# Linear attention and a one-expert MoE on one Trainium2 core: attention of each sequence placed about one MoE ahead of its own, w1 slot copy split over f, a weight load no longer ordered behind the last copies

## The chip, the cores and the metric

The kernel runs on one core of a Trainium2 chip. The metric is device time in microseconds of one execution. Engines are named as in the profile: PE does the matrix products (PEld its weight loads), DVE, ACT and POOL the elementwise work, SP issues transfers. A transfer issued from SP shows in the profile as queue q1, one from POOL as q0.

## What is computed

Eight sequences of 576 positions, eight heads of 64. The attention is linear (softmax over the features of q, softmax over the positions of k), and its result is the input of a mixture of experts in which one expert is chosen for each whole sequence:

```python
q_s = softmax(q, axis=-1)
k_s = softmax(k, axis=positions)
kv  = einsum('bhsd,bhse->bhde', k_s, v)
x   = einsum('bhsd,bhde->bhse', q_s, kv)          # -> (8, 576, 512)
logits = x.mean(axis=1) @ w_gate                  # 8 experts
e = argmax(logits); gate = softmax(logits)[e]     # one expert for each sequence
out = gate * (relu(x @ w1[e]) @ w2[e])            # w1 512x1024, w2 1024x512
```

For the inputs of these runs the experts of the eight sequences are 2, 3, 3, 1, 3, 3, 4, 6.

## The kernel before

**Halves and steps.** Attention is done in halves: half n belongs to sequence b = n // 2 and holds four heads, as two groups g of two heads each. For a half, ACT takes exp of q and k (`exp_q`, `exp_k`, L124, L136), POOL casts v to fp16 (`cast_v`, L132), DVE sums q over the features and takes the reciprocals (`scale_q`, L142, L144), and POOL multiplies them in (L145; DVE for the first halves). `kvt_step` then runs on PE the 18 small products of k and v (L160) and 18 transposes of q (L181). DVE takes both out of PSUM (`kv_out`, L168 and L170; `t_out`, L189). `x_step` multiplies them for one group (L219, L220), and one DVE instruction takes the result out and sums it for the gate (L230). There is one PSUM buffer for these products, which the gate's small products use too, so each x step waits until DVE has read the one before.

**Gate and weights.** `gate_step` (L261) multiplies the pooled x with w_gate (L265), and DVE finds the expert and whether one of the last sequences had it (L270 to L297). There are five slots for weights, and sequence b owns slot b % 5. POOL reads the expert's number and issues four transfers from the fp32 weights in DRAM to the fp16 slot: two for w1 (L315) and two for w2 (L327). Where the expert lies in a slot already, their condition is false and they move nothing. `gate_exp`, `gate_split` and `gate_spread` make the gate's weight and bring it to all partitions (L343, L348 to L351, L359 to L362). `fetch` (L365) copies, on DVE, the slot that holds the expert into the slot of the sequence, in two parts for w1 and two for w2 (L374); where the weights were just loaded it copies the slot onto itself. So for each sequence the MoE's weights pass through these four copies.

**The MoE.** `moe(b)` (L384) is a Python generator of 17 units. Units 0 to 7 make 128 rows of the hidden layer each (L393 for 512 positions, L398 for the other 64; ACT applies relu, L402). Units 8 to 15 are the four output tiles of 128 positions in two pieces each (L412), and ACT multiplies by the gate (L419). Unit 16 is the last 64 positions (L427).

**What sets the order.** Every engine runs its instructions in the order in which the program writes them (`manual_schedule`). A table of ticks sets it: sequence b's MoE takes ticks 17 b to 17 b + 17, one for each unit, and an entry `at(t, ...)` with t from 17 b + m up to 17 b + m + 1 is written right behind unit m of `moe(b)`. Attention of sequence 0, and of 1 but for two x steps, is written ahead of all MoEs. For b from 2 on, the table puts `kvt_step` of its two halves at two places, the x steps 2 and 4 ticks later, `exp_q` and `cast_v` 5.4 ticks ahead, `exp_k` and the input load of half n + 3 4.4 ahead, and `scale_q` 4.2 ahead. The gate follows the second half. The input tiles have three buffers, so the load of half n + 3 waits for the exps and the cast of half n. SP issues those loads and the stores of the output, in order.

Of the kernel before, what the change touches and what calls it, by code (L numbers as in the profile page):

```python
# [19 lines left out]
def kernel(  # L20
# [15 lines left out]
    nc = tc.nc  # L36
# [9 lines left out]
    NS = 5  # L46
# [61 lines left out]

    out_p = out.rearrange("b (p j) d -> b p j d", j=J)

    ins, halves, seqs, issued = {}, {}, {}, {}

    def load(n, names="qkv"):
        if n >= 2 * B:
# [19 lines left out]
    def exp_k(n):  # L134
        ek = e_pool.tile([128, J, 2, Dh], FP16, name="ek")
        nc.scalar.activation(out=ek.rearrange("p j n d -> p n j d"), in_=ins.pop((n, "k")), func=AF.Exp)  # L136
        halves[n]["ek"] = ek
# [123 lines left out]
    def gate_step(b):  # L261
# [103 lines left out]
    def fetch(b, w_all, part):  # L365

        if "src" not in seqs[b]:
            seqs[b]["src"] = nc.values_load(
                seqs[b]["sidx"][0:1, 0:1], engines=[ET.DVE], min_val=0, max_val=NS - 1,
                skip_runtime_bounds_check_because=IN_RANGE,  # L370
            )
        half = w_all.shape[2] // 2
        cs = slice(part * half, (part + 1) * half)
        copy = nc.vector.tensor_copy(  # L374
            out=w_all[:, b % NS, cs],
            in_=w_all[:, ds(seqs[b]["src"], 1), cs].rearrange("p o c f -> p (o c) f"),
        )
        for load_inst in issued.get(b + 1, ()):
            tc.declare_no_dep(
                copy.ins, load_inst.ins,  # L380
                reason="the slot that b + 1 loads into is taken out of the history before b looks for its source",
            )

    def moe(b):  # L384
        xt = seqs[b]["xt"]
# [72 lines left out]
    at_gate(2, 1)  # L458
    for b in range(2, B):
        u = 20 if b == 2 else 33 + 14 * (b - 3)  # L460
        for i in range(2):
            n, t = 2 * b + i, u + i * (8 if b == 2 else 5)
            at(t, kvt_step, n)
            for g in range(2):
                at(t + 2 + 2 * g, x_step, n, g)
            at(t - 5.4, exp_q, n)
            at(t - 5.4, cast_v, n)
            at(t - 4.4, exp_k, n)
            if n + 3 < 2 * B:
                at(t - 4.4, load, n + 3)  # L470
            at(t - 4.2, scale_q, n, nc.gpsimd)
# [23 lines left out]
    with tc.manual_schedule(engines={ET.PE, ET.DVE, ET.Activation, ET.Pool, ET.SP}):  # L495
# [75 lines left out]
```

## Time and profile before

| what | value |
|---|---|
| median of three runs | 228.77 us (226.83 to 229.58) |
| the profiled execution, its own time | 228.89 us |
| its span | 227.2 us |
| PE, DVE, ACT, POOL busy | 181.5, 118.0, 112.9, 60.6 us |
| PE idle before the hidden layer's products (L393), put down to DVE's copies (L374) | 18.4 us in 6 waits |
| weight transfers (q0), moved | 10.49 MB, five experts of 2.1 MB in fp16 |
| input loads and stores (q1), moved | 37.76 MB |

The span is what the profile shows between the first and the last instruction; the execution's own time is 1.7 us longer. Only sequences 0, 1, 3, 6 and 7 move weights. A row of the timeline gives the start in us, the time from its first to its last instruction, the engine and line, and in brackets how long the engine sat idle before it and what ended that.

### The profile page before, as it was taken

The page shows a single profiled execution, that of the slowest core. Times are in us where ns is not written, and L with a number is a line of the kernel's source. Part 1 is how long each engine was busy: PE and PEld are TensorE (multiplying, and loading weights), DVE is VectorE, ACT ScalarE, POOL GpSimd, SP SyncE. Part 2 cuts the span into 40 slices and gives each one's busy share as a digit, 9 for nine tenths or more (in the row PEclk, how much of TensorE's full clock was granted, in tenths as well). Part 3 has the DMA queues.
Part 4 walks back from the last instruction along what each step waited for, and adds up shares of the span by engine and source line. Part 5 has one row for each costly group of instructions (what it writes and reads, how often), then busy time and mean ns, then how long its engine had stood idle before and what let it go on. Part 6 is the DMA issues. An engine that isn't in the chain of part 4 may idle for free.

```text
span 227.2 us, 4594 instructions
## 1 busy us (share of the span) xinstructions
PE 181.5 (80%) x1703; PEld 96.1 (42%) x1703; DVE 118.0 (52%) x365; ACT 112.9 (50%) x177; POOL 60.6 (27%) x70
## 2 busy tenths in 40 slices
PE   6376599958999399965393996969898978999990
PEld 6353345423555145432151444544445533545440
DVE  0848824043548965673244876777699655220000
ACT  3785755462595134662035462845538432645541
POOL 1235403330254150267000334045137313000000
PEclk9755569996999769988599799999999996999999
DMA  6997999999999990399995569372425999965044
GB/s 201 379 390 283 145 251 297 183 235 351 398 400 401 373 316 4 100 300 201 289 285 142 198 182 282 109 264 52 106 54 75 194 250 183 208 122 131 0 107 102
DMA packets 28582, 48.55 MB, mean 214 GB/s; under 512 B 2960, under 2 KB 10128, under 8 KB 28560
## 3 DMA queue, kind: packets, MB, share of 16 engines
q1 hardware_dynamic: 19472, 37.76, 49.9%
q0 software_dynamic: 8544, 10.49, 28.5%
q8 instruction: 13, 0.21, 0.4%
q10 hardware_dynamic: 544, 0.02, 0.1%
q14 instruction: 9, 0.07, 0.1%
HBM read 61.88 MB, written 9.44 MB: 314 GB/s over the span
## 4 chain that ended last, share of the span: by engine, by line
PE 43%; DVE 22%; DMA 20%; ACT 5%; issue 5%; POOL 1%; DVEq 1%; POOLq 0%; ACTq 0%
DMA w_all<-in_moe_w_dram 16%; PE mm L393 16%; PE mm L412 15%; DVE qs L142 5%; DVE w_all L374 4%; PE kv L160 3%; DVE same L279 2%; PE x L219 2%; ACT eq L124 2%; PE ht L398 2%; DMA k_in<-in_k_dram 2%; DVE kv L170 2%; DMA q_in<-in_q_dram 2%; PE mm L427 2%; DVE xt L230 2%
## 5 line engine op out<-in xcount | busy, mean ns | idle before, releaser
L393 PE MATMUL mm<-xt,w_all 128*128 128x512 f16 x256 | 74.3, 421 | 18.9 <-DVE w_all L374 18.4
L402 ACT ACTIVATE hsb<-mm 128x512 f16<-128x512 f32 x64 | 37.6, 593 | 56.8 <-PE mm L393 56.7
L412 PE MATMUL mm<-w_all,hsb 128*128 128x512 f16 x256 | 60.9, 385 | 0.1
L145 POOL TENSOR_TENSOR eq<-eq,qsi 128x1152 f16<-128x1152 f16 x13 | 27.5, 2116 | 72.8 <-DVE zz L270 39.0
L393 PEld LDWEIGHTS <-w_all 128*128 128x128 f16 x256 | 21.7, 104 | 43.0 <-DVE w_all L374 23.5
L419 ACT ACTIVATE osb<-mm,gate 128x512 f32<-128x512 f32 x32 | 21.9, 684 | 29.3 <-PE mm L412 25.3
L412 PEld LDWEIGHTS <-hsb 128*128 128x128 f16 x256 | 23.5, 99 | 27.0 <-issue 1.7
L374 DVE COPY w_all<-w_all 128x2048 f16 x28 | 21.1, 754 | 22.4 <-DMA w_all<-in_moe_w_dram 21.3
L142 DVE TENSOR_REDUCE qs<-eq 128x18 f32<-128x1152 f16 x16 | 21.5, 1346 | 13.9 <-ACT eq L124 13.9
L230 DVE CUSTOM_DVE_ANT_0 xt<-x,ones_f 128x576 f16<-128x576 f32 x26 | 19.4, 746 | 18.0 <-PE x L220 18.0
L398 PEld LDWEIGHTS <-w_all 128*128 128x128 f16 x256 | 17.7, 104 | 18.2 <-issue 5.6
L132 POOL CAST va<-v_in 128x1152 f16<-128x1152 f32 x14 | 16.3, 1162 | 21.9 <-DMA v_in<-in_v_dram 21.7
L124 ACT ACTIVATE eq<-q_in 128x1152 f16<-128x1152 f32 x16 | 18.5, 1156 | 2.1 <-DMA q_in<-in_q_dram 2.0
L219 PE MATMUL x<-qt,kv 128*128 128x512 f16 x32 | 14.5, 452 | 6.2 <-DVE pooled L230 4.3
L398 PE MATMUL ht<-xt,w_all 128*128 128x64 f16 x256 | 19.2, 201 | 0.0
L136 ACT ACTIVATE ek<-k_in 128x1152 f16<-128x1152 f32 x16 | 18.5, 1158 | 0.8 <-DMA k_in<-in_k_dram 0.8
L315 POOL DMA_DIRECT2D w_all<-in_moe_w_dram x18 | 8.3, 463 | 31.0 <-DVE hl L350 24.1
L160 PEld LDWEIGHTS <-ek 64*128 64x128 f16 x288 | 10.4, 105 | 11.8 <-issue 8.0
L160 PE MATMUL kv<-va,ek 64*128 64x129 f16 x270 | 12.1, 236 | 2.7 <-ACT qt L187 2.3
L168 DVE RECIPROCAL icv<-kv 128x1 f32<-128x1 f32 x30 | 4.9, 162 | 13.1 <-PE kv L181 11.9
L170 DVE SCALAR_TENSOR_TENSOR kv<-kv,icv,blkmask 128x128 f16<-128x128 f32 x30 | 10.5, 351 | 1.1
L189 DVE COPY qt<-kv 128x576 f16<-128x576 f16 x24 | 10.7, 448 | 0.0
(80 smaller groups left out, 138.2 us busy)
## 6 DMA issues: line engine op xcount, KB each, us to landing
w_all<-in_moe_w_dram POOLq DMA_DIRECT2D x30, 512.0 KB
q_in<-in_q_dram SPq DMA_DIRECT2D x16, 576.0 KB, 7.0
k_in<-in_k_dram SPq DMA_DIRECT2D x16, 576.0 KB, 9.4
v_in<-in_v_dram SPq DMA_DIRECT2D x16, 576.0 KB, 9.1
out_dram<-osb SPq DMA_DIRECT2D x64, 128.0 KB, 5.1
w_all<-in_moe_w_dram POOLq DMA_DIRECT2D x4, 256.0 KB
out_dram<-osb_t SPq DMA_DIRECT2D x16, 64.0 KB, 3.3
wg_sb<-in_moe_w_gate_dram ACTq DMA_DIRECT2D x2, 8.0 KB, 5.1
```

The source lines that it names most:

```text
L124: nc.scalar.activation(out=eq.rearrange("p j n d -> p n j d"), in_=ins.pop((n, "q")), func=AF.Exp)
L142: nc.vector.tensor_reduce(out=qs, in_=eq, op=ALU.add, axis=AX.X)
L145: eng.tensor_tensor(out=eq, in0=eq, in1=qsi.unsqueeze(3).to_broadcast([128, J, 2, Dh]), op=ALU.mult,)
L160: nc.tensor.matmul(kps[g][:, 0:129], lhsT=ek[r, j], rhs=va[r, j], start=(j == 0), stop=(j == J - 1),)
L219: nc.tensor.matmul(px[:, 0:SM], lhsT=kvs[g], rhs=qts[g][:, 0:SM], start=True, stop=True)
L230: nc.vector.tensor_tensor_reduce(out=xt[:, c, :], in0=px[:, 0:S], in1=ones_f32.to_broadcast([128, S]), scale=1.0, scalar=0.0, op0=ALU.mult ...
L374: copy = nc.vector.tensor_copy(out=w_all[:, b % NS, cs], in_=w_all[:, ds(seqs[b]["src"], 1), cs].rearrange("p o c f -> p (o c) f"),)
L393: nc.tensor.matmul(phm, lhsT=w1_sb[:, c, fsl], rhs=xt[:, c, 0:SM], start=(c == 0), stop=(c == ND - 1),)
L398: nc.tensor.matmul(pht[:, fc * ST:(fc + 1) * ST], lhsT=w1_sb[:, c, fsl], rhs=xt[:, c, SM:S], start=(fc == 0 and c == 0), stop=(fc == NF - ...
L402: nc.scalar.activation(out=hsb[:, fc, 0:SM], in_=phm, func=AF.Relu)
L412: nc.tensor.matmul(po, lhsT=hsb[:, fc, st * 128:st * 128 + 128], rhs=w2_sb[:, fc, :], start=(fc == 0), stop=(fc == NF - 1),)
L419: nc.scalar.mul(osb, po, gate)
```

## The change

The table of ticks is written anew. The places of `kvt_step` for b = 2 to 7 go from (20, 28), (33, 38), (47, 52), (61, 66), (75, 80), (89, 94) to (15, 25), (30, 35), (41, 46), (58, 64), (74, 80), (91, 97). The MoEs of these sequences stay at ticks 34, 51, 68, 85, 102 and 119. The gate goes from 5 to 5.5 ticks behind the second half, and its three later steps from 1, 2 and 4 ticks behind it to 3, 4 and 6. The input loads of halves 5 and 6 go from tick 14 to 9.5. The copies of w2 go from 1 and 2 ticks behind the MoE's start to 4 and 5. In the copies of w1 the two parts are now the two halves of the hidden layer (f), where they were the two halves of the input features (c). The weight loads of sequence b are declared free of the copies of b - 1, where the program writes those copies first. Ahead of the MoEs, `exp_k(2)` goes ahead of an x step.

```diff
+        for load_inst in issued[b]:
+            for copy in copies.get(b - 1, ()):
+                apart(load_inst, copy)
+
+    def apart(first, second):
+        tc.declare_no_dep(
+            first.ins, second.ins,
+            reason="the slot that b + 1 loads into is taken out of the history before b looks for its source",
+        )
...
-        half = w_all.shape[2] // 2
-        cs = slice(part * half, (part + 1) * half)
+        if w_all is w1_all:
+            cs, fs = slice(0, ND), slice(part * (F // 2), (part + 1) * (F // 2))
+        else:
+            cs, fs = slice(part * (NF // 2), (part + 1) * (NF // 2)), slice(0, D)
         copy = nc.vector.tensor_copy(
-            out=w_all[:, b % NS, cs],
-            in_=w_all[:, ds(seqs[b]["src"], 1), cs].rearrange("p o c f -> p (o c) f"),
+            out=w_all[:, b % NS, cs, fs],
+            in_=w_all[:, ds(seqs[b]["src"], 1), cs, fs].rearrange("p o c f -> p (o c) f"),
         )
+        copies.setdefault(b, []).append(copy)
...
         at(t, gate_step, b)
-        at(t + 1, gate_exp, b)
-        at(t + 2, gate_split, b)
-        at(t + 4, gate_spread, b)
+        at(t + 3, gate_exp, b)
+        at(t + 4, gate_split, b)
+        at(t + 6, gate_spread, b)
...
+    at(9.5, load, 5)
+    at(9.6, load, 6)
+    places = [(15, 25), (30, 35), (41, 46), (58, 64), (74, 80), (91, 97)]
     for b in range(2, B):
-        u = 20 if b == 2 else 33 + 14 * (b - 3)
         for i in range(2):
-            n, t = 2 * b + i, u + i * (8 if b == 2 else 5)
+            n, t = 2 * b + i, places[b - 2][i]
...
-        at_gate(t + 5, b)
+        at_gate(places[b - 2][1] + 5.5, b)
     for b in range(1, B):
         for part in range(2):
-            at(NU * b - 0.8 + 0.2 * part, fetch, b, w1_all, part)
-            at(NU * b + 1 + part, fetch, b, w2_all, part)
-    at(14, load, 5)
-    at(14, load, 6)
+            at(NU * b - 1 + 0.5 * part, fetch, b, w1_all, part)
+            at(NU * b + 4 + part, fetch, b, w2_all, part)
...
         exp_q(2)
+        exp_k(2)
         x_step(1, 0)
-        exp_k(2)
         x_step(1, 1)
```

**On DVE, ahead of the copies of w1 for sequence 2.** Before, DVE ends that sequence's gate (nmx is its last instruction) and takes half 6 out of PSUM (icv, kv and qt for two groups) before it reads the slot's number (sidx) and copies:

```order
L297 TENSOR_SCALAR nmx_1148<-mx8_1132 1x1
L168 RECIPROCAL icv_1198<-kv_1160 128x1
L170 SCALAR_TENSOR_TENSOR kv_1200<-kv_1160,icv_1198,blkmask_93 128x128
L189 COPY qt_1202<-kv_1160 128x576
L168 RECIPROCAL icv_1204<-kv_1161 128x1
L170 SCALAR_TENSOR_TENSOR kv_1206<-kv_1161,icv_1204,blkmask_93 128x128
L189 COPY qt_1208<-kv_1161 128x576
L368 TENSOR_LOAD sidx_1144
L374 ISA
L374 COPY w1_all_119<-w1_all_119 128x2048
```

Now half 6 stands ahead of the gate, and between the gate and the copies stand the sums and reciprocals of half 7 (qs, qsi), whose product POOL then makes, and one x step of half 6 (xt):

```order
L297 TENSOR_SCALAR nmx_1164<-mx8_1148 1x1
L142 TENSOR_REDUCE qs_1184<-eq_1080 128x18
L144 RECIPROCAL qsi_1186<-qs_1184 128x18
L230 ISA xt_1202,pooled_1203<-x_1204,ones_f32_97 128x576
L230 ISA pooled_1203 128x1
L377 TENSOR_LOAD sidx_1160
L385 ISA
L385 COPY w1_all_119<-w1_all_119 128x4x512
```

What moved: kv and qt went ahead of the gate, and a sum with its product and an x step came in behind it, directly ahead of the copies.

**On SP, from the output of the first MoE on.** Before, the stores of three tiles (osb) go first, and then the inputs of halves 5 and 6:

```order
L421 DMA out_0_dram<-osb_717 64x512 x2
L421 DMA out_0_dram<-osb_730 64x512 x2
L421 DMA out_0_dram<-osb_743 64x512 x2
L119 DMA q_in_752<-in_q_dram 128x2x576
L119 DMA k_in_754<-in_k_dram 128x2x576
L119 DMA v_in_756<-in_v_dram 128x2x576
L119 DMA q_in_758<-in_q_dram 128x2x576
```

Now the inputs of halves 5, 6 and 7 follow the first tile, ahead of the other stores:

```order
L430 DMA out_0_dram<-osb_717 64x512 x2
L119 DMA q_in_721<-in_q_dram 128x2x576
L119 DMA k_in_723<-in_k_dram 128x2x576
L119 DMA v_in_725<-in_v_dram 128x2x576
L119 DMA q_in_727<-in_q_dram 128x2x576
L119 DMA k_in_729<-in_k_dram 128x2x576
L119 DMA v_in_731<-in_v_dram 128x2x576
L119 DMA q_in_743<-in_q_dram 128x2x576
L119 DMA k_in_745<-in_k_dram 128x2x576
L119 DMA v_in_747<-in_v_dram 128x2x576
L430 DMA out_0_dram<-osb_758 64x512 x2
```

What moved: nine loads stand behind two stores, where six stood behind six.

**On DVE, around the gate of sequence 3, whose weights have to be loaded.** Before, the sums of half 8 stand directly ahead of the gate's chain (zz to same), so POOL's product of half 8 and this chain start together:

```order
L230 ISA pooled_1259 128x1
L142 TENSOR_REDUCE qs_1410<-eq_1390 128x18
L144 RECIPROCAL qsi_1412<-qs_1410 128x18
L270 TENSOR_SCALAR zz_1428<-x_1423 1x8
L272 MAX mx8_1430<-zz_1428 1x8
L274 MAX_INDEX eidx_1432<-mx8_1430,zz_1428 1x8
L279 TENSOR_TENSOR same_1434<-hist_103,eidx_1432 1x8
```

Now those sums come earlier, and the copies of w2 for sequence 2 lie between the x steps that the gate needs:

```order
L142 TENSOR_REDUCE qs_1344<-eq_1318 128x18
L144 RECIPROCAL qsi_1346<-qs_1344 128x18
L230 ISA xt_1202,pooled_1203<-x_1359,ones_f32_97 128x576
L230 ISA pooled_1203 128x1
L385 ISA
L385 COPY w2_all_120<-w2_all_120 128x2048
L230 ISA xt_1202,pooled_1203<-x_1384,ones_f32_97 128x576
L230 ISA pooled_1203 128x1
L385 ISA
L385 COPY w2_all_120<-w2_all_120 128x2048
L270 TENSOR_SCALAR zz_1404<-x_1399 1x8
```

What moved: the sum no longer stands next to the gate, and a copy of w2 now stands behind the sum and between the x steps.

More of the change, by code (lines that the diff above doesn't have):

```diff
@@ L109 @@
     out_p = out.rearrange("b (p j) d -> b p j d", j=J)
-    ins, halves, seqs, issued = {}, {}, {}, {}
+    ins, halves, seqs, issued, copies = {}, {}, {}, {}, {}
     def load(n, names="qkv"):
@@ L371, in fetch @@
             )
-        half = w_all.shape[2] // 2
-        cs = slice(part * half, (part + 1) * half)
+        if w_all is w1_all:
+            cs, fs = slice(0, ND), slice(part * (F // 2), (part + 1) * (F // 2))
+        else:
+            cs, fs = slice(part * (NF // 2), (part + 1) * (NF // 2)), slice(0, D)
         copy = nc.vector.tensor_copy(
-            out=w_all[:, b % NS, cs],
-            in_=w_all[:, ds(seqs[b]["src"], 1), cs].rearrange("p o c f -> p (o c) f"),
+            out=w_all[:, b % NS, cs, fs],
+            in_=w_all[:, ds(seqs[b]["src"], 1), cs, fs].rearrange("p o c f -> p (o c) f"),
         )
+        copies.setdefault(b, []).append(copy)
         for load_inst in issued.get(b + 1, ()):
[L379 to L382, printed above, removed]
+            apart(copy, load_inst)
     def moe(b):
@@ L465 @@
                 at(t + 2 + 2 * g, x_step, n, g)
[L466 to L468 removed]
+            at(t - 5.35, exp_q, n)
+            at(t - 5.35, cast_v, n)
+            at(t - 4.35, exp_k, n)
             if n + 3 < 2 * B:
[L470 to L472 removed]
+                at(t - 4.35, load, n + 3)
+            at(t - 4.25, scale_q, n, nc.gpsimd)
+        at_gate(places[b - 2][1] + 5.5, b)
     for b in range(1, B):
         for part in range(2):
[L475 to L478 removed]
+            at(NU * b - 1 + 0.5 * part, fetch, b, w1_all, part)
+            at(NU * b + 4 + part, fetch, b, w2_all, part)
     times = sorted(ticks)
```

## The prediction

> **What bounds the kernel now.** I read the waits first, then PE's timeline, since PE is the busiest engine and the last one to finish.
>
> ```profile
> PEld L393 <- DVE w_all L374: 23.5, 12, 6.5
> DVE w_all L374 <- DMA w_all<-in_moe_w_dram: 21.3, 6, 5.9
> ```
>
> The hidden layer waits for DVE's copies, and these wait for weights. PE's timeline shows where:
>
> ```profile
> 47.41 1.06 PE L427 MATMUL mm<-w_all,hsb 128*64 128x256 f16 x16
> 52.11 1.55 PE L393 MATMUL mm<-xt,w_all 128*128 128x512 f16 x4 [3.63 <-DVE w_all L374]
> ...
> 63.41 3.62 PE L412 MATMUL mm<-w_all,hsb 128*128 128x512 f16 x16
> ...
> 78.07 1.89 PE L393 MATMUL mm<-xt,w_all 128*128 128x512 f16 x4 [3.56 <-DVE w_all L374]
> ...
> 99.36 0.16 PE L359 MATMUL x<-hl,ones_row 1*128 1x2 f16 x1 [2.15 <-DVE hl L351]
> ...
> 111.38 1.89 PE L393 MATMUL mm<-xt,w_all 128*128 128x512 f16 x4 [6.26 <-DVE w_all L374]
> ...
> 123.99 0.38 PE L219 MATMUL x<-qt,kv 128*128 128x512 f16 x1 [3.54 <-DVE pooled L230]
> ...
> 140.97 1.33 PE L393 MATMUL mm<-xt,w_all 128*128 128x512 f16 x4 [1.63 <-DVE w_all L374]
> ...
> 152.13 0.16 PE L359 MATMUL x<-hl,ones_row 1*128 1x2 f16 x1 [1.97 <-DVE hl L351]
> ...
> 165.19 1.33 PE L393 MATMUL mm<-xt,w_all 128*128 128x512 f16 x4 [1.47 <-DVE w_all L374]
> ...
> 188.13 1.33 PE L393 MATMUL mm<-xt,w_all 128*128 128x512 f16 x4 [1.85 <-DVE w_all L374]
> ...
> 193.17 1.03 PE L393 MATMUL mm<-xt,w_all 128*128 128x512 f16 x4
> ...
> 206.07 1.04 PE L393 MATMUL mm<-xt,w_all 128*128 128x512 f16 x4
> ...
> 213.92 7.07 PE L412 MATMUL mm<-w_all,hsb 128*128 128x512 f16 x32
> ...
> 220.92 1.06 PE L427 MATMUL mm<-w_all,hsb 128*64 128x256 f16 x16
> ```
>
> The rows in which L393 follows DVE are the starts of MoEs 1 to 6; 206.07 is MoE 7. Call them T1 to T7. The last MoE is alone on PE: 206.07 to 221.98, 15.9 us, 0.98 for a unit of the hidden layer and 0.88 for a piece of output. Before the others PE idles 1.5 to 6.3 us. Two more kinds of wait are inside MoEs: the gate's weight (99.36, 152.13), and 123.99, where DVE stood at a copy of w2 for which no weights were there. After most of the longer waits products run at half speed for a while (1.89 instead of 1.04); from 188.13 to 193.17 three units took 5.0 instead of 3.0 us. I charge 2.2 for such a restart, between 2.0 there and the 2.8 that 78.07 shows in its first three units.
>
> Prices of the pieces that move:
>
> ```profile
> 60.97 0.38 PE L219 MATMUL x<-qt,kv 128*128 128x512 f16 x1
> 61.21 1.03 PE L393 MATMUL mm<-xt,w_all 128*128 128x512 f16 x4
> ...
> 158.47 0.70 PE L160 MATMUL kv<-va,ek 64*128 64x129 f16 x18
> 159.37 1.90 PE L412 MATMUL mm<-w_all,hsb 128*128 128x512 f16 x8
> ```
> ```profile
> 73.65 0.15 DVE L270 TENSOR_SCALAR zz<-x 1x8 f32<-1x8 f32 x1 [0.50 <-PE x L265]
> 75.42 0.14 DVE L168 RECIPROCAL icv<-kv 128x1 f32<-128x1 f32 x1
> ...
> 132.14 0.17 DVE L168 RECIPROCAL icv<-kv 128x1 f32<-128x1 f32 x1 [0.55 <-PE kv L181]
> 133.80 1.34 DVE L142 TENSOR_REDUCE qs<-eq 128x18 f32<-128x1152 f16 x1
> 135.43 0.69 DVE L230 CUSTOM_DVE_ANT_0 xt<-x,ones_f 128x576 f16<-128x576 f32 x1
> ```
>
> From start to start, a half costs PE 0.9 us for products and transposes and 0.24 for each of two x steps; it costs DVE 1.66 to take them out, 1.63 for sums and reciprocals, and some 0.75 for each x step. A gate's chain costs DVE 1.77. And one collision:
>
> ```profile
> 49.39 2.11 POOL L145 TENSOR_TENSOR eq<-eq,qsi 128x1152 f16<-128x1152 f16 x1 [7.02 <-ACT ek L136]
> 127.01 2.12 POOL L145 TENSOR_TENSOR eq<-eq,qsi 128x1152 f16<-128x1152 f16 x1 [19.80 <-DVE zz L270]
> ```
> ```profile
> 49.97 2.81 DVE L374 COPY w_all<-w_all 128x2048 f16 x2 [0.76 <-DMA w_all<-in_moe_w_dram]
> ...
> 127.35 1.79 DVE L279 TENSOR_TENSOR same<-hist,eidx 1x8 f32<-1x8 f32 x1
> ```
>
> POOL's product ran to 51.50 and to 129.13. The two copies took 2.8 us (a pair takes 1.4 at other places), and a comparison of eight numbers lasted 1.79, to 129.14. So a copy, or this step of a gate, that meets POOL's product waits for its end.
>
> **The change, by the start of each MoE.**
>
> *T1.* The attention of half 4 now runs ahead of unit 16 of MoE 0, so PE ends that MoE at 48.47 + 0.9, near 49.3. What starts MoE 1 is w1, which landed at 49.9 (the copy above). Its load meets the inputs earlier:
>
> ```profile
> 43.05 4.83 SPq L421 DMA_DIRECT2D out_dram<-osb  x6
> ```
> ```profile
> q0 software_dynamic: 321, 0.34, 114.2%
> ```
> ```profile
> q0 software_dynamic: 233, 0.23, 71.2%
> ```
>
> The first q0 row is 45 to 47 us, with weights alone: 0.17 MB/us. The second is 49 to 51, with inputs beside them: 0.115. Six stores took 4.8 us, and the inputs waited behind them to 47.9; behind two stores they flow from about 45.5. So the 2.4 us to 47.9 go at 0.115 instead of 0.17 and take 3.5: w1 lands at 51.0. The copy is then free of POOL, whose product is done by 48, and PE needs only the first part: T1 = 51.8 (bounds 50.7, no slowing, and 53). The Trainium skill (DMA: Bandwidth & Descriptors, Queues, rings and completion order) says that the engines take turns between queues packet by packet; an even split, 0.085, would make T1 53.0, and the 0.115 measured here decides against it.
>
> *T2.* Before, PE took 11.3 us from T1 to the first output piece (63.41), with one half's products and two x steps inside; without the 0.9, 62.3. Then six pieces (5.3), halves 5 and 6 (1.8), two x steps and a short wait for DVE between them (0.9) bring half 6 to its end at 70.3. On DVE follow: half 6 out (1.66), the gate's chain (1.77), sums of half 7 (1.63), an x step (0.75): 76.1. PE has finished MoE 1 by 73.6. At 75.4 POOL starts half 7's product, so the copy waits to 77.5 and more: it ends 0.6 behind the product as at 49.97, at 78.5 with 0.3 for POOL's start. T2 = 78.5, nothing won against 78.07 (bounds 76.8 without the collision, 80). This is DVE's queue, not the weights: sequence 2 moves none.
>
> *T3.* From T2: the MoE 15.9, halves 7 to 9 2.7, seven x steps 1.7, 2.2 for the slow restart, and a rest of 1.3. That rest is MoE 4 before: 24.2 from 140.97 to 165.19, less 15.9, two halves, six x steps (1.44), and 1.97, 1.47 and 0.3 of waits, gives 1.6; 0.3 of it goes since PE no longer stops for the second part of w1 (first unit 1.33 against 1.04). New waits: the gate behind an x step that stands behind a w2 copy that meets POOL's product (1.5); the transposes of half 9 for their product (1.35); the copy behind the x step directly ahead of it, as at 165.19 (1.5). Together 28.2: T3 = 106.7, against 111.38. Are the weights there?
>
> ```profile
> 99.18 1.36 POOL L315 DMA_DIRECT2D w_all<-in_moe_w_dram  x2 [1.74 <-DVE hl L350]
> 186.85 1.37 POOL L315 DMA_DIRECT2D w_all<-in_moe_w_dram  x2 [8.34 <-DVE hl L350]
> ```
> ```profile
> 97.87 0.14 DVE L289 TENSOR_SCALAR fresh<-top 1x1 uint32<-1x1 f32 x1
> ...
> 110.63 1.42 DVE L374 COPY w_all<-w_all 128x2048 f16 x2 [5.88 <-DMA w_all<-in_moe_w_dram]
> 121.84 1.42 DVE L374 COPY w_all<-w_all 128x2048 f16 x2 [3.88 <-DMA w_all<-in_moe_w_dram]
> ...
> 196.88 1.42 DVE L374 COPY w_all<-w_all 128x2048 f16 x2 [3.59 <-DMA w_all<-in_moe_w_dram]
> 202.10 1.43 DVE L374 COPY w_all<-w_all 128x2048 f16 x2 [3.80 <-DMA w_all<-in_moe_w_dram]
> ```
>
> From issue, w1 took 11.4 us beside inputs and 10.0 without, w2 22.6 and 15.2. POOL issued 1.2 behind the end of L289. In the new order the gate of sequence 3 issues 15.6 behind T2 (seven units 6.9, restart 2.2, half 7 and three x steps 1.6, the wait of 1.5, gate product and second w2 copy 0.7, chain to L289 1.5, POOL 1.2), near 94.1 instead of 99.18; w1 lands by 105.5, just ahead of its copy.
>
> *T4.* 15.9, two halves 1.8, three x steps 0.7, rest 1.3, copy behind an x step that runs beside unit 16: 0.6. And w2: it lands 15.2 to 22.6 behind 94.1, at 109 to 117; its copies stand ahead of the gate's weight on DVE, which PE wants at 114 and POOL's product of half 10 can hold to 115. I take 2.4 (bounds 0, and 4 with a slow restart of 2.2). 22.7: T4 = 129.4, against 140.97. Here most of the gain lies: 6.26, 3.54 and their restarts, and 2.15 before it, are gone or smaller, and a half is done earlier.
>
> *T5, T6.* 15.9, 1.8, five or four x steps (1.2, 1.0), 1.3, and 1.5 at the next start: 21.7 and 21.5. T5 = 151.1, T6 = 172.6. The gate's wait (1.97) goes, since its chain no longer meets POOL's product and its weight has two ticks more.
>
> *T7 and the end.* The gate of sequence 7 now follows T6. Its issue is 4.7 behind it (two units, chain, 1.2 to POOL), w1 lands 10 later and is copied at T6 + 15.4. MoE 6 takes 15.9 + 0.7: T7 = 189.2, a margin of 1.2 (at 11.4 it is gone, and costs 0.2). From T7 on nothing changes: 227.2 - 206.07 = 21.1, so the span ends at 210.3.
>
> **Edits at nothing.** Freeing loads from the last copies: before, those copies were over long before the issue (99.18); now the gate's chain stands behind them on DVE anyway. Without that cover it is a copy, 0.7. `exp_k(2)` earlier: PE's first output pieces wait for w2 of sequence 0, which moves no earlier.
>
> The profiled execution took 228.89 for its span of 227.2, 1.7 more, and the median is 228.77: no difference. 210.3 + 1.7 = **212.0 us**.
>
> **A rule that bears on the sum.** Half speed followed waits of 3.5 us and more, but 1.85 (188.13) too, and did not follow 1.97 (152.13). The Trainium skill (TensorE: Matmul & The Clock Gate, What's actually happening) has the clock fall only after a whole idle window of about 3.4 us, free-running. By that, my waits of 2.4 to 2.5 at T1 and in MoE 3 cost no restart and the sum stands; by the 188.13 row each would add 2.0, and it is 216.
>
> **Rivals.** *All of it hides* (0.16): POOL's product does not meet the copy at T2 (-1.7) and w2 of sequence 3 is there in time (-2.4): 208. For it: sequence 3's load has fewer inputs beside it. Against it: DVE's chain at T2 is 5.8 us long with POOL's product at its end. *The weights come late* (0.18): inputs run beside all of sequence 1's and 3's loads. T1 +1.2, w2 at 117 holds DVE so that PE's wait grows from 2.4 to 4 and restarts slowly (+1.6, +2.2), sequence 7's w1 +0.2: 217; with the restart at T1 219. *POOL and DVE set the pace* (0.05, the other side): each transpose waits for its half's product, because DVE is behind with its sums. Between ticks 25 and 51 DVE has some 32 us of work (five halves out 8.3, four sums 6.5, ten x steps 7.5, two gates with their weights 5.3, six copies 4.2), and PE has 26 units, 24.5, with five halves and ten x steps, 6.9: as much. If this costs one product (2.12) at each of 12 halves, that is 25 less the 1.35 counted: 236. It turns slower than before from 8 of 12 halves on (16.8 of lead over 2.12). *The order has no such effect* (0.03): MoE 3's weights land no sooner than 110.6 and 121.8, because the inputs pulled ahead hold the queue. T3 and the waits of MoE 3 then stay, T4 is earlier by the half and x steps already done (1.6), and the rest follows as above, 80.9 behind it: 222.
>
> **Chances and range.** Forecast 0.58, then as given. The range runs from the first rival with 3 off for T2's and T3's lower bounds to the late weights with the restart and 2 more: 205 to 221. Two per cent, 4.6 us, is what a measurement can tell here: faster, below 224.2, has the first three cases less their tails, 0.90; within, 0.06; slower, 0.04.
>
> **What would show it.** T1 near 52, T2 near 78.5 behind a copy stretched by POOL's product, T3 near 107 with about 1.5 idle, no L359 behind hl for 2 us, T4 near 129, T7 near 189. Wrong: T3 at 111 or later, PE at half speed more than four times after T1, or transposes (L181) waiting for L145 at most halves.

## The result and the profile after

The change runs in 215.79 us, median of 4 runs (215.02 to 218.3), against 229.18 (226.83 to 229.66) for the kernel before beside it: ratio 0.9424, 95% interval 0.9336 to 0.9511. Timed again beside three of the experiments it gave 216.53 us against 228.1, 0.9537 (0.9477 to 0.9597). The comparisons here leave disturbed runs out, so a ratio need not be the quotient of the medians beside it.

The profiled execution took 215.46 us, its span 213.7. On the page of the changed kernel, the busy time of the engines and the group of DVE's copies (busy, mean ns of one, idle before):

```profile
PE 176.0 (82%) x1703; PEld 94.3 (44%) x1703; DVE 119.0 (56%) x365; ACT 113.3 (53%) x177; POOL 62.2 (29%) x70
...
L385 DVE COPY w_all<-w_all 128x2048 f16 x28 | 29.5, 1052 | 14.0 <-DMA w_all<-in_moe_w_dram 13.7
```

The span is 13.5 shorter. PE's busy time fell from 181.5 to 176.0, and the rest of the span from 45.7 to 37.7. PE has nearly the same products to do, so the 5.5 are for the most part products that no longer run at half speed; 4.4 of them are at the hidden layer's products for 512 positions (74.3 to 69.9). The waits of the changed kernel (us in total, times, longest):

```profile
PEld L402 <- DVE w_all L385: 14.5, 6, 5.1
DVE w_all L385 <- DMA w_all<-in_moe_w_dram: 13.7, 5, 6.0
```

They stood at 23.5 in 12 waits and 21.3 in 6. PE's timeline of the changed kernel, in the rows that answer to those of before:

```profile
51.03 1.04 PE L402 MATMUL mm<-xt,w_all 128*128 128x512 f16 x4 [1.84 <-DVE w_all L385]
...
59.37 1.03 PE L421 MATMUL mm<-w_all,hsb 128*128 128x512 f16 x4
...
75.96 1.89 PE L402 MATMUL mm<-xt,w_all 128*128 128x512 f16 x4 [4.79 <-DVE w_all L385]
...
88.49 0.35 PE L265 MATMUL x<-wg_sb,pooled 128*1 128x8 f32 x8 [1.51 <-DVE pooled L230]
...
98.00 0.44 PE L181 MATMUL kv<-ident,eq 64*128 64x64 f16 x18 [1.19 <-POOL eq L145]
...
105.89 1.04 PE L402 MATMUL mm<-xt,w_all 128*128 128x512 f16 x4 [2.74 <-DVE w_all L385]
...
107.26 1.75 PE L402 MATMUL mm<-xt,w_all 128*128 128x512 f16 x4
...
109.04 1.89 PE L402 MATMUL mm<-xt,w_all 128*128 128x512 f16 x4
...
115.82 0.16 PE L368 MATMUL x<-hl,ones_row 1*128 1x2 f16 x1 [0.83 <-DVE hl L360]
...
128.61 1.04 PE L402 MATMUL mm<-xt,w_all 128*128 128x512 f16 x4 [0.47 <-DVE w_all L385]
...
151.14 1.04 PE L402 MATMUL mm<-xt,w_all 128*128 128x512 f16 x4 [1.47 <-DVE w_all L385]
...
159.66 0.70 PE L160 MATMUL kv<-va,ek 64*128 64x129 f16 x18 [1.11 <-POOL va L132]
161.74 0.44 PE L181 MATMUL kv<-ident,eq 64*128 64x64 f16 x18 [1.37 <-POOL eq L145]
162.22 1.89 PE L402 MATMUL mm<-xt,w_all 128*128 128x512 f16 x4
...
176.41 1.04 PE L402 MATMUL mm<-xt,w_all 128*128 128x512 f16 x4 [1.47 <-DVE w_all L385]
...
192.84 1.04 PE L402 MATMUL mm<-xt,w_all 128*128 128x512 f16 x4
```

Read as a ledger, from the start of one MoE to the next (us):

| stretch | before | predicted | after |
|---|---|---|---|
| start to T1 | 52.1 | 51.8 | 51.0 |
| T1 to T2 | 26.0 | 26.7 | 24.9 |
| T2 to T3 | 33.3 | 28.2 | 29.9 |
| T3 to T4 | 29.6 | 22.7 | 22.7 |
| T4 to T5 | 24.2 | 21.7 | 22.5 |
| T5 to T6 | 22.9 | 21.5 | 25.3 |
| T6 to T7 | 17.9 | 16.6 | 16.4 |
| T7 to the end | 21.1 | 21.1 | 20.9 |

Of the 13.5 us, 10.3 are won between T2 and T4, 2.3 are lost again in MoE 5, and the other stretches give 5.6 together.

### The profile page after: what moved, and what is told of

The parts are those of the page before. It is cut to its first block, busy times and chain, and to the rows that moved or that the text cites. A ratio compares the mean times of both kernels' runs of the same rounds, so it can differ in the third digit from the quotient of the medians.

```text
span 213.7 us, 4597 instructions
## 1 busy us (share of the span) xinstructions
PE 176.0 (82%) x1703; PEld 94.3 (44%) x1703; DVE 119.0 (56%) x365; ACT 113.3 (53%) x177; POOL 62.2 (29%) x70
## 4 chain that ended last, share of the span: by engine, by line
PE 43%; DMA 25%; DVE 19%; issue 5%; POOL 3%; ACT 1%; DVEq 1%; POOLq 0%; ACTq 0%
PE mm L421 19%; DMA w_all<-in_moe_w_dram 17%; PE mm L402 15%; DVE w_all L385 7%; DMA v_in<-in_v_dram 5%; DVE qs L142 4%; DMA wg_sb<-in_moe_w_gate_dram 3%; PE kv L160 2%; PE mm L436 2%; PE x L219 2%; PE ht L407 2%; DVE kv L170 2%; DVE qt L189 2%; DVE xt L230 1%; PE kv L181 1%
## 5 line engine op out<-in xcount | busy, mean ns | idle before, releaser
L402 PE MATMUL mm<-xt,w_all 128*128 128x512 f16 x256 | 69.9, 405 | 12.8 <-DVE w_all L385 12.8
L385 DVE COPY w_all<-w_all 128x2048 f16 x28 | 29.5, 1052 | 14.0 <-DMA w_all<-in_moe_w_dram 13.7
L402 PEld LDWEIGHTS <-w_all 128*128 128x128 f16 x256 | 21.4, 102 | 34.8 <-DVE w_all L385 14.5
L145 POOL TENSOR_TENSOR eq<-eq,qsi 128x1152 f16<-128x1152 f16 x13 | 28.0, 2152 | 26.6 <-DVE qsi L144 25.5
L421 PEld LDWEIGHTS <-hsb 128*128 128x128 f16 x256 | 23.3, 98 | 26.2 <-issue 0.8
L142 DVE TENSOR_REDUCE qs<-eq 128x18 f32<-128x1152 f16 x16 | 21.5, 1343 | 10.1 <-ACT eq L124 10.1
L132 POOL CAST va<-v_in 128x1152 f16<-128x1152 f32 x14 | 17.7, 1261 | 24.7 <-DMA v_in<-in_v_dram 24.6
L407 PEld LDWEIGHTS <-w_all 128*128 128x128 f16 x256 | 17.0, 101 | 17.1 <-issue 3.3
L407 PE MATMUL ht<-xt,w_all 128*128 128x64 f16 x256 | 18.6, 197 | 0.0
L219 PE MATMUL x<-qt,kv 128*128 128x512 f16 x32 | 14.0, 438 | 2.7 <-DVE kv L170 0.8
L181 PE MATMUL kv<-ident,eq 64*128 64x64 f16 x270 | 7.3, 196 | 7.6 <-POOL eq L145 3.0
```

The lines of the kernel that those rows point to most:

```text
L142: nc.vector.tensor_reduce(out=qs, in_=eq, op=ALU.add, axis=AX.X)
L145: eng.tensor_tensor(out=eq, in0=eq, in1=qsi.unsqueeze(3).to_broadcast([128, J, 2, Dh]), op=ALU.mult,)
L385: copy = nc.vector.tensor_copy(out=w_all[:, b % NS, cs, fs], in_=w_all[:, ds(seqs[b]["src"], 1), cs, fs].rearrange("p o c f -> p (o c) f"),)
L402: nc.tensor.matmul(phm, lhsT=w1_sb[:, c, fsl], rhs=xt[:, c, 0:SM], start=(c == 0), stop=(c == ND - 1),)
L407: nc.tensor.matmul(pht[:, fc * ST:(fc + 1) * ST], lhsT=w1_sb[:, c, fsl], rhs=xt[:, c, SM:S], start=(fc == 0 and c == 0), stop=(fc == NF - ...
L421: nc.tensor.matmul(po, lhsT=hsb[:, fc, st * 128:st * 128 + 128], rhs=w2_sb[:, fc, :], start=(fc == 0), stop=(fc == NF - 1),)
```

## The experiments

Each of them computes the whole result. Three questions were open. First, which part carries the gain: my theory was the places of the attention, together with the later copies of w2; the rival, that the split of w1 or the freed load does it by itself. Then, what MoE 5 lost: POOL's queue, or DVE's, which I had costed. Last, what the hour of the weights' issue is worth: in the prediction T3 rests on an earlier issue of sequence 3's weights; the rival is that the inputs ahead of them decide. A short name stands ahead of each experiment; T1 to T7 are the starts of MoEs 1 to 7 in its profile.

**c split: the change with the copies of w1 split over c again.**

```diff
-        if w_all is w1_all:
-            cs, fs = slice(0, ND), slice(part * (F // 2), (part + 1) * (F // 2))
-        else:
-            cs, fs = slice(part * (NF // 2), (part + 1) * (NF // 2)), slice(0, D)
+        half = w_all.shape[2] // 2
+        cs, fs = slice(part * half, (part + 1) * half), slice(0, w_all.shape[3])
```

> The changed kernel with the two copies of w1 split over c again. Theory (the split over f is a small term of its own): PE stops again for the second part, 0.3 us at each of six starts of a MoE, and at MoE 2, where POOL's work holds both copies, by up to 1.2 more: 217.5 to 219 us against 215.8. In the trace the first unit of a MoE takes 1.3 instead of 1.04. Rival (the split does nothing, since the copies are over before PE asks): 215.8.

Measured: 218.68 us (216.29 to 219.62) against 228.64, ratio 0.9508 (0.942 to 0.9596). PE of this kernel, where in the changed kernel the first unit takes 1.04 and has no second wait:

```profile
79.07 1.03 PE L400 MATMUL mm<-xt,w_all 128*128 128x512 f16 x2 [0.53 <-DVE w_all L383]
...
107.16 1.33 PE L400 MATMUL mm<-xt,w_all 128*128 128x512 f16 x4 [1.75 <-DVE w_all L383]
```

The row at 79.07 is the other half of MoE 2's first unit, which waits for the second part of w1; 107.16 is T3, with 0.3 for it, as at three later starts. By these rows the split over f is worth 0.3 at most starts and 0.5 at T2. The ratio alone does not prove it, since its interval overlaps that of the change, and the profiled run also starts MoE 1 at half speed (1.76 at 50.99) and waits 3.24 for the gate's weight in MoE 3, where the change has 1.04 and 0.83; no run shows whether the split has a part in these.

**Ordered loads: the change with the weight loads ordered behind the last copies again.**

```diff
-        for load_inst in issued[b]:
-            for copy in copies.get(b - 1, ()):
-                apart(load_inst, copy)
```

> The changed kernel with the weight loads ordered behind the last copies again. Theory: nothing, since the copies of w2 for sequence 2 end at 89.0 and the loads of sequence 3 issue at 91.7 behind a gate's chain that DVE runs after them: 215.8 us within noise, issue of the loads of 3, 6 and 7 unmoved. Rival (the wait was there): issue of sequence 3's loads later by 0.5 us or more, and the time by 1 to 3.

Measured: 217.28 us (215.76 to 218.32), ratio 0.9489 (0.9422 to 0.9555). The first transfer for sequence 3 is issued at 92.71, 3.25 behind the start of the gate's product at 89.46; in the changed kernel it is 91.74, also 3.25 behind 88.49. The freedom changes nothing there, as the prediction had it: the gate's chain stands behind those copies on DVE in either case.

**Old places: the table of before for attention, gates and loads; the split, the later w2 copies and the freedom kept.**

```diff
-    at(9.5, load, 5)
-    at(9.6, load, 6)
-    places = [(15, 25), (30, 35), (41, 46), (58, 64), (74, 80), (91, 97)]
+    at(14, load, 5)
+    at(14.1, load, 6)
+    places = [(20, 28), (33, 38), (47, 52), (61, 66), (75, 80), (89, 94)]
...
-        at_gate(places[b - 2][1] + 5.5, b)
+        at_gate(places[b - 2][1] + 5, b)
```

> The changed kernel with the table of places, the gate's steps and the loads of halves 5 and 6 of the kernel before; the split over f, the later copies of w2 and the freed loads stay. Theory (the placement carries the gain, by the weights of sequence 3): the loads of sequence 3 issue near 98 again, MoE 3 starts near 110, 225 to 228 us. Rival (split, later w2 copies or freed loads carry it): 221 us or less.

Measured: 225.35 us (223.84 to 227.91), ratio 0.9797 (0.9736 to 0.9858). PE starts MoE 3 in it so:

```profile
109.58 1.89 PE L402 MATMUL mm<-xt,w_all 128*128 128x512 f16 x4 [5.25 <-DVE w_all L385]
```

The wait at T3 is there again, with its restart at half speed. What is left of the gain is about 2%, with an interval of 1.4 to 2.6%.

**Places only: the places of the change, but w1 split over c, w2 copied at +1 and +2, loads ordered.**

```diff
-            at(NU * b + 4 + part, fetch, b, w2_all, part)
+            at(NU * b + 1 + part, fetch, b, w2_all, part)
```

(and the edits of the first two experiments)

> The kernel before with the new places, gate steps and loads alone: split over c, copies of w2 1 and 2 ticks behind the start, loads ordered behind the last copies. Theory: most of the gain, 219 to 222 us: 3 from the split over c, and DVE stands at the copy of w2 of sequence 3 from near 109 to 114, so that half 10's product and the gate's weight come late, 1 to 3. Rival (the placement is worth little alone): 226 us or more.

Measured: 222.16 us (220.9 to 222.23), ratio 0.9687 (0.9635 to 0.9739). In its MoE 3 PE waits for the gate's weight:

```profile
120.48 0.16 PE L365 MATMUL x<-hl,ones_row 1*128 1x2 f16 x1 [5.19 <-DVE hl L357]
```
```profile
116.93 1.42 DVE L380 COPY w_all<-w_all 128x2048 f16 x2 [5.97 <-DMA w_all<-in_moe_w_dram]
```

DVE stands 5.97 at the copy of w2, which has not landed, and the weight is queued behind it: MoE 3 takes 27.1 from T3 to T4 instead of 22.7 (23.5 in the repetition below). So the later copies of w2 are worth some 4 us here. Old places and places only together multiply to 0.949, near the two ratios of the whole change: the parts are close to additive. The places carry some 60% of it. The rest falls, as far as these rows tell, for the most part to the later w2 copies, since the kernels without the other two edits stand near the change; no run moves the w2 copies alone.

**The same again: the changed kernel, on the chip of the next three.**

> The changed kernel once more, beside the three that follow. 214.5 to 217.5 us; MoE 6 starts some 25 us behind MoE 5 and MoE 2 some 25 behind MoE 1.

Measured: 216.53 us (215.66 to 218.2), ratio 0.9537 (0.9477 to 0.9597). T3 is 107.40, behind a wait of 3.83, and the gate's weight costs 1.79 in MoE 3. Half 14 has the same two waits, 1.11 and 1.37, but no product of MoE 5 runs at half speed behind them, and it takes 24.2 instead of 25.3.

**Gate 6 later: the gate of sequence 6 at tick 86.8.**

```diff
-        at_gate(places[b - 2][1] + 5.5, b)
+        at_gate(86.8 if b == 6 else places[b - 2][1] + 5.5, b)
```

> The changed kernel with the gate of sequence 6 at tick 86.8 instead of 85.5, so that POOL casts v and multiplies half 14 ahead of the weight loads of sequence 6. Theory (POOL's 3.3 us of issuing these loads held half 14): both waits of PE at half 14 (1.1 and 1.4) and the half speed behind them go, MoE 5 takes 21.5 to 22.5 us instead of 25.3, and the time falls by 3: 212.5. The gate's comparison on DVE then meets POOL's product (1.8), which nobody waits for. Rival (DVE's sums or the input of half 14 were late): MoE 5 stays near 25.

Measured: 217.66 us (214.87 to 219.52), ratio 0.9547 (0.9478 to 0.9616): no gain. The two waits at half 14 are gone, but another came. DVE and then PE of this kernel:

```profile
157.01 1.80 DVE L279 TENSOR_TENSOR same<-hist,eidx 1x8 f32<-1x8 f32 x1
```
```profile
164.98 0.39 PE L219 MATMUL x<-qt,kv 128*128 128x512 f16 x1 [2.36 <-DVE gate L371]
```

The gate's chain now meets POOL's product (1.80 for eight numbers), everything on DVE is later, and the gate's weight is read out of the one PSUM buffer of the x steps only behind the sums of half 15, which start at 163.00. The x step waits 2.36 for that buffer. The place was right and the time was not: a gate moved as a whole takes its DVE work with it.

**Copy 2 early: the w1 copies of sequence 2 right behind its gate's chain.**

```diff
-            at(NU * b - 1 + 0.5 * part, fetch, b, w1_all, part)
+            at(30.6 + 0.02 * part if b == 2 else NU * b - 1 + 0.5 * part, fetch, b, w1_all, part)
```

> The changed kernel with the two copies of w1 for sequence 2 directly behind its gate's chain, ahead of the sums of half 7. Theory (POOL's product and cast held these copies): the two copies take 1.4 us instead of 4.2, MoE 2 starts 3 to 4 us earlier, at 72 to 73, at full speed or with a shorter slow start; half 7 then waits up to 2 us for its product. Time down by 2 to 4: 212 to 214. Rival (DVE was simply behind, and the copies only showed it): MoE 2 starts at most 1.5 earlier and the time stays within 1.

Measured: 214.36 us (213.91 to 217.22), ratio 0.9432 (0.9377 to 0.9487). PE, then DVE, of this kernel at T2:

```profile
73.26 1.04 PE L402 MATMUL mm<-xt,w_all 128*128 128x512 f16 x4 [1.80 <-DVE w_all L385]
...
76.24 0.58 PE L219 MATMUL x<-qt,kv 128*128 128x512 f16 x1 [1.82 <-DVE pooled L230]
```
```profile
72.52 1.42 DVE L385 COPY w_all<-w_all 128x2048 f16 x2 [1.10 <-DMA w_all<-in_moe_w_dram]
```

The copies take 1.42 instead of 4.18 and PE waits 1.80 instead of 4.79, so it was the sums, the x step and POOL's work that made it wait; how much each of them did, this edit doesn't tell. Of the 1.80, 1.10 is DVE waiting for transfers that move nothing: POOL issues the two for w1 at 71.94 and 72.41. T2 is 3.5 earlier than in the repetition, but the x step that is now late waits 1.82, with a restart behind it, and T3 is only 1.6 earlier. T4 is 3.4 earlier, because MoE 3 has no wait for the gate's weight here (1.79 there). MoE 5 is 1.1 longer, at half speed, and the end 2.4 earlier.

**Both: the last two edits together.**

```diff
-        at_gate(places[b - 2][1] + 5.5, b)
+        at_gate(86.8 if b == 6 else places[b - 2][1] + 5.5, b)
...
-            at(NU * b - 1 + 0.5 * part, fetch, b, w1_all, part)
+            at(30.6 + 0.02 * part if b == 2 else NU * b - 1 + 0.5 * part, fetch, b, w1_all, part)
```

> Both of these edits. If they are separate losses they add up: 5 to 7 us below the changed kernel, 209 to 211. If one gives back the other (weights of sequence 3 or inputs as the next bound): no more than 3 below.

Measured: 213.53 us (211.07 to 214.4), ratio 0.9355 (0.9277 to 0.9434). POOL issues sequence 3's weights at 88.68, three us earlier than in the change. The queues of this kernel from 88 to 93 (packets, MB, share of 16 engines):

```profile
q1 hardware_dynamic: 907, 1.93, 100.8%
q0 software_dynamic: 12, 0.02, 2.6%
```

The inputs fill the engines and the weights move next to nothing. w1 lands at 103.2, 14.6 behind its issue, and T3 still waits 3.94, where 1.47 is what the copy alone costs. The two expected gains don't add up: T2, T3 and T4 are 3.8, 3.4 and 3.4 earlier than in the repetition, which is copy 2, and MoE 5 with 23.7 keeps nearly all that it lost.

**Gate 3 later: the gate of sequence 3, and with it its weights, at tick 43.**

```diff
-        at_gate(places[b - 2][1] + 5.5, b)
+        at_gate(43 if b == 3 else places[b - 2][1] + 5.5, b)
```

> The changed kernel with the gate of sequence 3 at tick 43, where the kernel before had it, instead of 40.5; all else as changed. Theory (the earlier issue of sequence 3's weights is what wins T3 and T4): issue later by some 3 us, near 95, and MoE 3's start and all behind it later by 2 to 4, 218 to 220 us. Rival (the weights come from a backlog of inputs, and the hour of their issue hardly matters): MoE 3 starts at most 1 later, 216 to 217.

Measured: 217.28 us (216.34 to 219.5), ratio 0.9552 (0.9477 to 0.9627). The issue on POOL and the copy on DVE in this kernel:

```profile
97.20 1.36 POOL L315 DMA_DIRECT2D w_all<-in_moe_w_dram  x2 [1.74 <-DVE pooled L230]
```
```profile
107.09 1.42 DVE L385 COPY w_all<-w_all 128x2048 f16 x2 [2.62 <-DMA w_all<-in_moe_w_dram]
```

Issued 5.5 later, the weights are there 1.95 later than in the change (105.14), and less than half a us later than in the repetition (106.65). T3 is 107.84, 1.95 and 0.44 later than in these two, and the time lies between what the theory and the rival gave. Against the repetition the rival holds, against the first profile it is near the least that the theory gave; what both show is that most of the later issue doesn't reach the landing. That the inputs hold the weights is what the next experiment tests.

**Load 12 later: the input load of half 12 at tick 51.5, behind MoE 3's start, instead of 41.65.**

```diff
-                at(t - 4.35, load, n + 3)
+                at(51.5 if n == 9 else t - 4.35, load, n + 3)
```

> The changed kernel with the inputs of half 12 loaded at tick 51.5 instead of 41.65, behind the start of MoE 3; they are needed at 68.65. Theory (inputs pulled ahead hold sequence 3's weights): w1 lands 1.5 to 2.5 us earlier, PE's wait ahead of MoE 3 falls from 2.7 to 3.8 to about 1.5, the wait for the gate's weight in MoE 3 (0.8 to 1.8) goes, time down by 1.5 to 3. Rival (weights are as slow alone): MoE 3's start and the time stay.

Measured: 212.36 us (211.16 to 212.43), ratio 0.9289 (0.9239 to 0.9338). The queues from 92 to 97 us, first of the changed kernel, then of this one, with issues at 91.74 and 92.35:

```profile
q1 hardware_dynamic: 579, 1.25, 79.6%
q0 software_dynamic: 92, 0.19, 20.5%
```
```profile
q0 software_dynamic: 261, 0.52, 64.1%
q1 hardware_dynamic: 35, 0.07, 4.4%
```

And its PE at T3 and T4:

```profile
105.22 1.04 PE L402 MATMUL mm<-xt,w_all 128*128 128x512 f16 x4 [1.47 <-DVE w_all L385]
...
125.37 1.04 PE L402 MATMUL mm<-xt,w_all 128*128 128x512 f16 x4 [0.47 <-DVE w_all L385]
```

One load of 1.7 MB out of the way and the weights move 2.7 times as much in those 5 us; the wait of 2.74 at T3 becomes 1.47, which is the copy behind its x step; no unit of MoE 3 runs at half speed, the gate's weight is not waited for, and MoE 3 takes 20.2 instead of 22.7. The wait at T3 alone would prove little: in the next experiment, with load 12 where the change has it, it is 1.58, and w2 is late instead (3.24 at the gate's weight). But from T2 to T4 this kernel takes 48.9, while the change, its repetition and the four other kernels that have this load, the split and the w1 copies of sequence 2 as in the change (ordered loads, gate 3 later, gate 6 later, loads 6 later) take 52.7 to 54.5.

**Loads 6 later: only POOL's issue of sequence 6's weights, at tick 87, behind half 14's product; the gate's chain stays.**

```diff
+        if b != 6:
+            gate_load(b)
+
+    def gate_load(b):
...
+    at(87, gate_load, 6)
```

> The changed kernel with only the issue of sequence 6's weight loads moved, from right behind its gate to behind half 14's product on POOL (tick 87); the gate stays at 85.5. Theory (POOL's issuing held half 14): both waits at half 14 go, no new one comes, since the gate's weight is made as before; MoE 5 takes 21.5 to 22.5 us instead of 24 to 25, time down by 2 to 3: 213 to 214. Rival (half 14 was late for another reason): MoE 5 unchanged.

Measured: 212.48 us (211.11 to 214.18), ratio 0.9297 (0.9217 to 0.9377). POOL, then PE, of this kernel:

```profile
158.15 2.43 POOL L145 TENSOR_TENSOR eq<-eq,qsi 128x1152 f16<-128x1152 f16 x1 [10.95 <-ACT hsb L417]
160.53 1.37 POOL L321 DMA_DIRECT2D w_all<-in_moe_w_dram  x2
```
```profile
160.61 0.70 PE L160 MATMUL kv<-va,ek 64*128 64x129 f16 x18
161.15 0.42 PE L181 MATMUL kv<-ident,eq 64*128 64x64 f16 x18
```

Half 14 has no wait, and no half speed follows; MoE 5 takes 21.4, which is what I had predicted for it (21.5). Nothing but the issue moved here, so the cause was POOL's queue.

**All three: copy 2 early, load 12 later, loads 6 later.**

```diff
-            at(NU * b - 1 + 0.5 * part, fetch, b, w1_all, part)
+            at(30.6 + 0.02 * part if b == 2 else NU * b - 1 + 0.5 * part, fetch, b, w1_all, part)
...
-                at(t - 4.35, load, n + 3)
+                at(51.5 if n == 9 else t - 4.35, load, n + 3)
...
+    at(87, gate_load, 6)
```

> The three edits together: copies of w1 for sequence 2 behind its gate, sequence 6's loads behind half 14's product, inputs of half 12 behind MoE 3's start. If the losses are separate: 208 to 211 us, MoE 3 from 102 to 103, MoE 5 in 22.

Measured: 209.54 us (209.0 to 211.0), ratio 0.9195 (0.9138 to 0.9253): it is faster than both kernels. Against the 216.5 of the repetition the three alone won 2.2, 4.2 and 4.0, together 7.0 and not 10.4. That timing is from another chip than the last two and this one; against the first 215.8 each is 0.7 less. PE of this kernel shows where some of it stays:

```profile
51.23 1.52 PE L408 MATMUL mm<-xt,w_all 128*128 128x512 f16 x4 [1.83 <-DVE w_all L391]
...
103.10 1.04 PE L408 MATMUL mm<-xt,w_all 128*128 128x512 f16 x4 [1.47 <-DVE w_all L391]
...
112.52 0.16 PE L374 MATMUL x<-hl,ones_row 1*128 1x2 f16 x1 [2.01 <-DVE hl L366]
```

T1 restarts at half speed this time, and with T3 at 103.1 w2 is late again for the gate's weight, which costs 2.01; the x step behind T2 waits its 1.82 as with copy 2 alone. So from T2 to T4 the later load wins 2.2 here (52.0, against 54.2 with copy 2 alone), where alone it won 4 or more.

## Why the prediction was right, and where it was not

The sum came out 3.4 below the span, and what it named was what happened: the long waits of MoE 2's end and of MoE 3 are gone, and nothing of their size took their place. But its single terms missed by -1.8 to +3.8, and some of the agreement is errors that cancel. One slip of arithmetic is in it: the rest of MoE 4, from the numbers given, is 1.3 before the 0.3 for the first unit is taken off, not 1.6 (the other 0.3 among its waits is an x step's, 0.28 at 157.26), so T3, T4, T5 and T6 each hold 0.3 too much, and the slip brought the forecast 1.2 nearer to the result.

**T1, 0.8 early.** DVE's copies in the changed kernel, at T1, T2, T3 and in MoE 3:

```profile
50.28 1.42 DVE L385 COPY w_all<-w_all 128x2048 f16 x2 [0.30 <-DMA w_all<-in_moe_w_dram]
...
73.28 4.18 DVE L385 COPY w_all<-w_all 128x2048 f16 x2
...
105.14 1.42 DVE L385 COPY w_all<-w_all 128x2048 f16 x2 [1.19 <-DMA w_all<-in_moe_w_dram]
...
114.19 1.09 DVE L385 COPY w_all<-w_all 128x2048 f16 x1 [1.74 <-DMA w_all<-in_moe_w_dram]
```

w1 landed just before 50.28, not at 51.0. POOL issued it at 37.01, and at 37.40 before, so it took 13.3 us from issue instead of 12.6: the inputs beside it cost about 0.7 instead of the 1.1 that I took from one window of the trace, and the rest is the earlier issue.

**T1 to T2, 1.8 shorter than predicted.** The collision came as told. POOL in the changed kernel:

```profile
71.65 0.05 POOL L315 DMA_DIRECT2D w_all<-in_moe_w_dram  x1 [3.28 <-DMA w_all<-in_moe_w_dram]
...
73.01 0.04 POOL L336 DMA_DIRECT2D w_all<-in_moe_w_dram  x1 [0.41 <-DMA w_all<-in_moe_w_dram]
73.23 2.12 POOL L145 TENSOR_TENSOR eq<-eq,qsi 128x1152 f16<-128x1152 f16 x1 [0.18 <-issue]
75.29 1.62 POOL L132 CAST va<-v_in 128x1152 f16<-128x1152 f32 x1
...
91.74 1.36 POOL L315 DMA_DIRECT2D w_all<-in_moe_w_dram  x2 [4.53 <-DVE kv L170]
...
155.12 1.51 POOL L315 DMA_DIRECT2D w_all<-in_moe_w_dram  x2 [11.14 <-DVE nmx L297]
156.90 1.55 POOL L336 DMA_DIRECT2D w_all<-in_moe_w_dram  x2 [0.27 <-issue]
158.44 1.17 POOL L132 CAST va<-v_in 128x1152 f16<-128x1152 f32 x1
159.56 2.12 POOL L145 TENSOR_TENSOR eq<-eq,qsi 128x1152 f16<-128x1152 f16 x1
```

The product starts at 73.23 and the copies last 4.18 instead of 1.42; PE starts on the first of them, 2.7 behind the product's start, where I had 3.1. The mis-sized term is "11.3 us from T1 to the first output piece": it was read off a stretch of before that held a restart at half speed (its first unit took 1.55), though the sum charged none at T1. With the half's 0.9 taken off, 10.4 was in the sum; now it is 8.3 from 51.03 to 59.37, with no slow unit.

**T2 to T3, 1.7 longer.** The three waits stand where they were put: 1.51 (predicted 1.5), 1.19 (1.35) and 2.74 (1.5). The last was too low because w1, issued at 91.74, landed 13.4 later and not 11.4. Here a reason of mine fell, though the sign came out right. I argued that the earlier issue brings the weights in time. The later gate shows that 5.5 us of issue time move the landing by 2 or less, and the later load shows what does more: the inputs that the change itself pulled ahead.

**T3 to T4, 22.7 for 22.7, by two errors.** The gate's weight cost 0.83 and not 2.4, and the wait at T3 was followed by a restart that the sum did not hold (107.26 and 109.04: 0.7 and 0.85 over 1.04, with the small products 1.8). w2 landed 22.4 behind its issue, at the upper end of the range given. In four other profiles with the same order up to there (the repetition, ordered loads, gate 6 later, loads 6 later) this wait was 1.79, 2.06, 0.80 and 3.24, so its size is not a property of the order; it hangs on when w2 lands and on whether its copies then meet POOL's product (one took 2.57 in the repetition). What the prediction lacked is a term of its own for the later copies of w2: it told the old stall at 123.99 as gone, and the places-only kernel shows that with copies at +1 and +2 it would have become 5.19 at the gate's weight.

**T4 to T5, 0.8 longer.** Two short waits, 0.27 at 137.18 and 0.34 at 140.11, are most of it.

**T5 to T6, 3.8 too short: the step that failed.** "T5, T6. ... 21.7 and 21.5" counted the earlier gate of sequence 6 on DVE alone. Its expert is new, so POOL has four transfers to issue, and in the new order they stand ahead of half 14's cast and product: 155.12 to 158.44 on POOL. The cast and the product follow at 158.44 and 159.56, and PE waits 1.11 and 1.37 for them and then runs at half speed from 162.22. In the repetition, without that half speed, the loss is 2.7. Before, the same issuing lay between half 14's product and half 15's cast, and PE wanted half 15 only 3 us behind its cast. A moved step had been followed through DVE and PE, but not through the queue in which it issues.

**T6 to the end** is right within 0.4.

**The rivals.** "All of it hides" fell at T2. "The weights come late" is true in part, at T3 (13.4 for w1) and not at T1. "POOL and DVE set the pace" did not come: the transposes wait over 1 us for a product at two halves (n = 9 and 14) and not at twelve of them. "The order has no such effect" is refuted by old places against the change.

**The clock.** In the changed kernel half speed follows the waits of 4.79 and 2.74, and the two of half 14, never 1.47. From T1 on, in all fourteen profiles, it follows each of the 21 waits of 3.4 us or more. Of the waits between 1.8 and 3.3 some were followed by it (1.83, 2.15, 2.74) and some were not (1.84, 2.37, 3.10); of two of 3.24 one was and one was not. Of shorter waits only those at half 14 were, where two stand within 3 us of each other, and there not in every profile. The Trainium skill (TensorE: Matmul & The Clock Gate, What's actually happening) asks for a whole idle window of about 3.4 us, in a window that runs freely. The runs agree with the free-running part, and with 3.4 as a length that was enough each time, but not as the least: the 1.84 at T1 is followed by full speed in the change (51.03, 1.04) and the 1.83 at the same place by 1.52 (51.23) in the last experiment. So the prediction's charge of one restart at T2, behind a wait of 4.8, held in all nine profiles with that wait; what it lacked is that waits of 2 to 3 us are a draw. The 216 that it named for restarts at T1 and at the gate's weight in MoE 3 lies near the 215.8 by luck: the profiled run had neither, and its restarts came behind T3 and half 14.

## What to carry to other kernels

Follow a step that is moved through every queue on which it leaves an instruction, transfers issued from a compute engine included: here 3.3 us of issuing ahead of a cast cost 2.7 to 3.8 us in one MoE, and moving the issue alone gave them back. Where a transfer is late, look at what fills the engines before you issue it earlier: taking one input load out of its way won some 4 us, and issuing it 5.5 us later made it land 2 us later at most. And before you read a duration off the old trace, see whether it holds a stall or a slow restart that the new order won't have.

## What was not expected of the hardware

POOL's casts block DVE's copies as its products do, and are stretched by them: two copies that take 1.42 alone took 4.18 beside a product and a cast, and the cast 1.62 instead of 1.17 (75.29 and 158.44). A single copy of w2 that meets only the end of a cast, at 115.69 in the changed kernel, took 1.16 instead of 0.69. The mean copy went from 754 to 1052 ns. The Trainium skill (SBUF — State Buffer, Who interferes with whom) says that the first of the two to start holds the shared ports for the whole instruction, which fits the order: product, copy, cast, copy, one after the other. By these durations that would be 4.7, and from the product's start to the end of the copies it was 4.2, so something of them overlaps.

Idle times of 1.8 us can cost some 1.7 us of half speed or nothing. At T1, behind the same wait, half speed followed in three of the twelve profiles with the new places, and T1 to T2 took 23.3 in the last experiment and 21.6 with copy 2 early alone. It may be one reason why runs of one kernel spread over 2 us and more; no run here separates it from others.

A load that moves nothing still holds POOL: the four transfers of sequence 2, whose condition is false, take 1.4 us there (71.65 to 73.05), beside 3.3 for four real ones (155.12 to 158.44), and with copy 2 early DVE's copies wait 1.10 for it. How much of the weights' slowness beside the inputs is the transfer engines' order and how much the time POOL takes to describe the transfers was not told apart.
